# An attention and MLP block on one core: the last MLP block's results kept on chip, the rest of y fetched into the room of queries and keys, x and attention output loaded further ahead

## The chip, the cores and the metric

The kernel runs on one core of a Trainium2 chip. The core has TensorE (PE, matmuls, with its weight loads shown as PEld), VectorE (DVE), ScalarE (ACT), GpSimd (POOL) and SyncE (SP), which here only issues transfers; 16 DMA engines carry these between device memory and the on-chip memory (SBUF). Matmuls write accumulators (PSUM). The metric is the device time of one execution in microseconds; the median of several runs counts.

## What is computed

```python
B, S, D, H, W, F = 1, 2048, 640, 32, 256, 1536          # 20 columns per head

def attention(x, wqkv, wo):
    qkv = (x @ wqkv).reshape(B, S, 3, H, D // H).transpose(2, 0, 3, 1, 4)
    q, k, v = qkv[0], qkv[1], qkv[2]
    scores = jnp.einsum("bhqd,bhkd->bhqk", q, k) * (D // H) ** -0.5
    mask = (i - j >= 0) & (i - j < W)                    # sliding window, i query, j key
    p = softmax(jnp.where(mask, scores, -1e9))
    o = jnp.einsum("bhqk,bhkd->bhqd", p, v)
    return o.transpose(0, 2, 1, 3).reshape(B, S, D) @ wo

def mlp(x, w1, b1, w2, b2):
    r = relu(x @ w1 + b1)
    return (r * r) @ w2 + b2

xn = layernorm(x)
out = x + attention(xn, wqkv, wo) * silu(mlp(xn, w1, b1, w2, b2))
```

All is float32. Every product is made of three matmuls in a reduced format: each operand is split into a high part and a rest, and high x high, high x rest and rest x high are summed.

## The kernel before

Rows of x come in 16 tiles t of 128 and in four blocks b of four tiles. A first phase normalises x, turns it, keeps the turned blocks in device memory (xs) and makes V and the first queries and keys. The rest runs under a hand-written order: whatever Python emits first stands first on its engine, and each engine works through its own list in that order.

**The attention loop** (`for s in range(steps)`) runs over 16 pairs of heads p and 16 tiles q, with lags for the second pass over the scores and for the values. Pair p uses the buffers `qs[p % 2]` and `ks[p % 2]`, each 128 x 2048; pair 15, the last, uses `qs1` and `ks1`, so `qs0` and `ks0` lie unused from the end of pair 14 on. Exponents of scores lie in eight buffers `p32`. What a pair gives is stored to device memory as `o_d[g]`, one for each of four groups g of query tiles, and the sums that it must be divided by stand in it as additional rows.

**The filler** (`filler`) is a generator whose matmuls are put between those of the attention, up to a pace (`fill`). It makes the remaining queries and keys, and then the MLP in eight blocks n = (hf, b): for hf = 0 the first half of F over all blocks b, stored as `y_d[0]`; for hf = 1 the second half, to which the first is added (`yin`, loaded from `y_d[0]`), stored as `y_d[1]`. The second half goes over the blocks 2, 3, 0 and 1; the last block (n == last) holds the tiles 4 to 7. Its eight accumulations (four tiles tt, two halves nh of 320 columns) are evicted by DVE into `ysb` (`evac`). Ahead of each of them `late(j)` is called, which loads attention output of unit 0, and, where the attention loop is over (`state[2]` is then 10 ** 6), does more.

**The output stage** (`out_filler`) follows with eight units u of two tiles each (`tile_of`: 0 and 2, 1 and 3, 4 and 6, 5 and 7, and so on). Unit u belongs to group g = u // 2 and needs

- the attention output `ob` of its 256 query columns and the reciprocals of the sums (`sums`), issued by `load(u)`: four transfers of 160 KB and one of 128 KB. The reciprocals are made by `invert`: the rows of sums of a group are loaded as `rec`, DVE inverts them, and they are stored to `rec_d[g]`;
- `turn_out(u, 0)`, in which DVE multiplies `ob` by `sums` and ACT copies it into the high part of `oT`, and `turn_out(u, 1)`, in which DVE subtracts to get the rest, each in two pieces (columns of chunks 0 and 1, then 2 to 4);
- y of its two tiles, `yb`, one transfer of 640 KB issued at the end of `load(u)`, over which ACT then applies Silu;
- x of its tiles, `xres`, 320 KB each (`load_res`), one tile ahead of use.

For each tile and each half nh, 15 matmuls `wops` (L599) run into one of the three accumulators mm0 to mm2, DVE multiplies them by y into `res` (`evac`), POOL adds x, and SP stores `res`. The matmuls of the first tile of unit u are emitted after the turning out of unit u + 1 has begun, so on DVE the multiplication for unit u + 1 stands ahead of the evictions of unit u.

SP issues all transfers from one list. In the built program every transfer is bound to one of eight semaphores in turn, and waits for the transfer eight places ahead of it to land; besides it waits for its data and its buffer.

Of the kernel before, what the change touches and what calls it, by code (L numbers as in the profile page):

```python
# [15 lines left out]
P = 128  # L16
# [41 lines left out]
def attn_mlp_kernel(ctx: ExitStack, tc, x, wqkv, wo, w1, b1, w2, b2, out):  # L58
# [56 lines left out]
    qs = [at.tile([P, S], F32R, name="qs0")]  # L115
    ks = [at.tile([P, S], F32R, name="ks0")]
# [293 lines left out]
    qs.append(at1.tile([P, S], F32R, name="qs1"))  # L410
    ks.append(at1.tile([P, S], F32R, name="ks1"))
# [415 lines left out]
    def filler():  # L827
# [50 lines left out]
        def late(j):  # L878
            load(0)
            if state[2] < 10 ** 6:  # L880
                return
            invert()
            start_pieces()
            for f in release(1, True):
                f()
                held[0] -= 1
            if j >= 5:
                turn_out(0, 0)
            if j >= 6:
                turn_out(0, 1)  # L890
                load(1)

        for n, (hf, b) in enumerate(blocks):
# [54 lines left out]
            for tt in range(4):  # L948
# [4 lines left out]
                def start(nh, hf=hf, t=t, place=place, idx=4 * (n - NB) + tt, end=n == NB - 1 and tt == 3, n=n, tt=tt):  # L953
# [3 lines left out]
                    def evac():  # L957
                        vload[0] += 0.5
                        if not nh:
                            place[0] = wgt.tile([P, D], F32, tag="wgqh", name="ysb")  # L960
# [3 lines left out]
                        if nh:  # L964
                            post(y_d[hf][:, t, :], ysb)
# [20 lines left out]
                for nh in range(2):  # L986
                    yield from room()
                    if n == last:
                        late(2 * tt + nh)
# [24 lines left out]
    def invert():  # L1014
        for g in range(NB):
            if state[2] < stored(g) + 3:
                return
            rows = o_d[g].rearrange("p (h r) n -> (p h) r n", h=2)
            if g not in recs:
                recs[g] = at2.tile([P, P], F32, tag="rec", name="rec")  # L1020
                for par in range(2):
                    nc.sync.dma_start(recs[g][64 * par:64 * (par + 1)], rows[:, 32 * par + DH].rearrange("h (j n) -> h j n", n=P))
                return
            if recs[g] is not None and state[2] >= stored(g) + 5:
                nc.vector.reciprocal(recs[g], recs[g])
                nc.sync.dma_start(rec_d[g].rearrange("a h (j n) -> (a h j) n", n=P), recs[g])
                recs[g] = None

    def load(u):
        if u in ld or u >= 2 * NB or recs.get(u // 2, 0) is not None:  # L1030
            return
        if u % 2 == 0:
            obs[u // 2] = [bigp.tile([P, KC * BT], F32, tag="big", name=f"{w}_{u // 2}") for w in ("ob", "yb")]
        ob, yb = (t_[:, u % 2 * 2 * D:(u % 2 + 1) * 2 * D] for t_ in obs[u // 2])
        ob, yb = ob.rearrange("p (c n) -> p c n", c=KC), yb.rearrange("p (t d) -> p t d", t=2)
        sums = at2.tile([P, MT], F32, tag="sums", name="sums")
# [4 lines left out]
        t = tile_of(u, 0)  # L1041
        nc.sync.dma_start(yb, y_d[1][:, t:t + 3:2, :])
        ld[u] = (ob, yb, sums)

    obs, oT, turned_out = {}, {}, set()

    def turn_out(u, part):
# [3 lines left out]
        ob, _, sums = ld[u]  # L1051
# [7 lines left out]
        else:  # L1059
            for cs in cuts:  # L1060
                nc.vector.tensor_sub(oT[u][:, 1, cs], ob[:, cs], f32(oT[u][:, 0, cs]))

# [11 lines left out]
    def out_filler(wo_part):  # L1074
        xts = {}

        def load_res(t):
# [145 lines left out]
```

## Time and profile before

| | |
|---|---|
| median of 3 runs | 876.19 us (874.11 to 877.67) |
| the profiled execution | 874.52 us, its span 872.8 us, mean granted TensorE clock 0.994 |
| PE busy | 851.0 us (98%) |
| PEld busy | 795.2 us (91%) |
| DVE, ACT, POOL busy | 447.5, 422.7, 319.7 us |
| moved by DMA | 169.11 MB, mean 194 GB/s |

The span is the time from the first to the last instruction of the profiled execution; the rest of its time lies around it. A row of the timeline gives the start and the length of a run of equal instructions in us, the engine, the line of the source, the operation, what it writes and reads, shape and count, and in brackets how long the engine was idle ahead of it and what ended that. A row of the stretches gives busy time and count of instructions for PE, PEld, DVE, ACT and POOL, the granted clock, the share of the DMA engines and GB/s. SPq is SP's queue: its rows are issues, not transfers.

### The profile page before, as it was taken

The numbers are of one execution on the slowest core, as the hardware profiler recorded it, in microseconds if no ns is written. First come the engines' busy times: TensorE is split into PE (matmuls) and PEld (weight loads), VectorE is DVE, ScalarE is ACT, GpSimd is POOL, SyncE is SP. The second block draws the span as 40 slices with busy tenths as digits, with TensorE's granted clock in tenths as the row PEclk, the third lists the DMA queues.
The fourth block names the chain that finished last, engine by engine and source line by source line (L and its number), as shares of the span: only waits on it lengthen the run. The fifth ranks groups of instructions, "written<-read, shape, count | busy, mean of one in ns | idle before, by whom it ended". The sixth has DMA issues, their size and how long they took to land.

```text
span 872.8 us, 26498 instructions
## 1 busy us (share of the span) xinstructions
PE 851.0 (98%) x10640; PEld 795.2 (91%) x10640; DVE 447.5 (51%) x1348; ACT 422.7 (48%) x800; POOL 319.7 (37%) x652
## 2 busy tenths in 40 slices
PE   9999999999999999999999999999999999999787
PEld 8999999888888999999999989999999999889786
DVE  7652146656567555454454466454454454235443
ACT  5222114545557744745735756735736636622221
POOL 6010002333333543543634533634534534403232
PEclk9999999999999999999999999999999999999999
DMA  7997587778789373273475255474474452478995
GB/s 269 297 401 285 174 222 251 255 255 265 246 266 308 91 227 106 62 231 94 115 213 160 66 170 160 140 219 121 133 239 114 144 192 75 105 192 220 243 254 171
DMA packets 95394, 169.11 MB, mean 194 GB/s; under 512 B 10920, under 2 KB 43816, under 8 KB 94248
## 3 DMA queue, kind: packets, MB, share of 16 engines
q1 hardware_dynamic: 95272, 167.42, 63.5%
q8 instruction: 84, 1.38, 0.7%
q14 instruction: 38, 0.31, 0.1%
HBM read 94.97 MB, written 71.83 MB: 191 GB/s over the span
## 4 chain that ended last, share of the span: by engine, by line
PE 87%; DMA 7%; DVE 2%; issue 2%; ACT 1%; POOL 1%; SPq 0%; DVEq 0%; POOLq 0%
PE yps L468 20%; PE hps L468 20%; PE qkps L468 14%; PE ops L546 10%; PE vps L228 8%; PE stps L518 5%; PE sps L478 4%; PE qkps L205 3%; DMA xres<-in_A_x_dram 2%; DMA sums<-rec 2%; DMA out_dram<-res 1%; DMA yb<-y 1%; PE wops L599 1%; PE tps L172 1%; POOL res L1121 1%
## 5 line engine op out<-in xcount | busy, mean ns | idle before, releaser
L486 DVE CUSTOM_DVE_ANT_0 junk<-sps,mask 128x384 bf16<-128x384 f32 (+2 forms) x512 | 272.6, 532 | 249.2 <-PE hps L468 72.7
L524 ACT ACTIVATE p<-stps 128x768 f32<-128x768 f32 (+2 forms) x256 | 197.3, 771 | 261.4 <-PE stps L518 211.4
L468 PE MATMUL yps<-w,hh 64*128 64x320 f32 x1536 | 231.0, 311 | 3.6 <-DVE ysb L962 3.2
L525 POOL TENSOR_SCALAR_AFFINE_SELECT p<-p 128x256 f32<-128x256 f32 x256 | 105.6, 412 | 334.2 <-ACT p L524 325.6
L468 PE MATMUL hps<-xb,w 64*128 64x256 f32 x2520 | 220.8, 283 | 0.0
L468 PEld LDWEIGHTS hps<-xb,w 64*128 64x128 f32 x2520 | 209.0, 187 | 5.5 <-issue 5.4
L468 PEld LDWEIGHTS yps<-w,hh 64*128 64x128 f32 x1536 | 186.5, 186 | 8.2 <-DVE ysb L962 4.7
L468 PE MATMUL yps<-w,hl 64*128 64x320 f32 x768 | 178.3, 311 | 0.0
L478 PE MATMUL sps<-ks,qs 60*128 60x384 f32 (+2 forms) x512 | 142.6, 341 | 0.3
L518 PE MATMUL stps<-qs,ks 62*128 62x384 f32 (+2 forms) x512 | 135.6, 332 | 0.0
L468 PEld LDWEIGHTS yps<-w,hl 64*128 64x128 f32 x768 | 117.3, 186 | 2.4 <-issue 2.3
L468 PE MATMUL qkps<-xT,wgkh 64*128 64x512 f32 x320 | 100.5, 395 | 0.0
L468 PE MATMUL qkps<-xT,wgqh 64*128 64x512 f32 x320 | 98.9, 393 | 0.0
L546 PE MATMUL ops<-p,vp 128*21 128x128 f32 (+1 forms) x2112 | 92.8, 313 | 0.0
L527 POOL TENSOR_SCALAR_AFFINE_SELECT p<-p 128x256 f32<-128x256 f32 x224 | 91.4, 408 | 0.0
L478 PEld LDWEIGHTS sps<-ks,qs 60*128 60x128 f32 x512 | 87.8, 185 | 2.6 <-DVE mt L486 1.3
L518 PEld LDWEIGHTS stps<-qs,ks 62*128 62x128 f32 x512 | 88.7, 188 | 0.4
L546 PEld LDWEIGHTS ops<-p,vp 128*21 128x21 f32 x2112 | 65.2, 100 | 22.1 <-issue 9.0
L599 PE MATMUL wops<-wo,oT 128*128 128x320 f32 x384 | 65.0, 319 | 11.6 <-DVE res L1116 9.5
L599 PEld LDWEIGHTS wops<-wo,oT 128*128 128x128 f32 x384 | 59.8, 195 | 13.6 <-DVE res L1116 10.6
L228 PE MATMUL vps<-wv,xT 128*128 128x320 f32 x480 | 71.5, 308 | 0.0
L228 PEld LDWEIGHTS vps<-wv,xT 128*128 128x128 f32 x480 | 70.5, 188 | 0.1
(100 smaller groups left out, 1160.0 us busy)
## 6 DMA issues: line engine op xcount, KB each, us to landing
ks<-k_d SPq DMA_DIRECT2D x64, 240.0 KB
qs<-q_d SPq DMA_DIRECT2D x64, 240.0 KB
xb<-xs SPq DMA_DIRECT2D x60, 256.0 KB
xs<-xT SPq DMA_DIRECT2D x8, 1280.0 KB
y<-ysb SPq DMA_DIRECT2D x32, 320.0 KB
k_d<-shm SPq DMA_DIRECT2D x19, 512.0 KB
q_d<-shm SPq DMA_DIRECT2D x19, 512.0 KB
o<-osb SPq DMA_DIRECT2D x64, 128.0 KB
```

The lines of the kernel that those rows point to most:

```text
L172: nc.tensor.transpose(ps[:, t * P:(t + 1) * P], xns[t][:, c * P:(c + 1) * P], ident)
L205: nc.tensor.matmul(ps, wt[:, c, :], xT[part][b][:, c * BT + t0:c * BT + t0 + n], start=m == 1, stop=m == 3 * KC)
L228: nc.tensor.matmul(ps, xT[xp][b][:, c * BT + t * P: c * BT + (t + 1) * P], wv[wp][:, c, nh * HALF:(nh + 1) * HALF], start=first and m == 0 ...
L468: return nc.tensor.matmul(out, a[r], b_[r], skip_group_check=True, **kw)
L478: nc.tensor.matmul(ss[hh][:, :nk], qs[i][o, q * P:(q + 1) * P], ks[i][o, k0 * P:k0 * P + nk], start=True, stop=True)
L486: nc.vector.tensor_tensor_reduce(out=junk[:, :nk], in0=ss[hh][:, :nk], in1=mask[:, 3 * P - nk:], scale=1.0, scalar=-3.0e38, op0=ALU.add, o ...
L518: nc.tensor.matmul(tps[:, hh, :n], ks[i][o, kb * P:(kb + 1) * P], qs[i][o, kb * P:kb * P + n], start=True, stop=True)
L524: nc.scalar.activation(p32[:, :, :n], tps[:, :, :n], AF.Exp, scale=SCALE)
L525: nc.gpsimd.affine_select(p32[:, :, 0:P], p32[:, :, 0:P], pattern=[[0, 2], [1, P]], compare_op=ALU.is_ge, fill=0.0, base=0, channel_multip ...
L527: nc.gpsimd.affine_select(p32[:, :, 2 * P:], p32[:, :, 2 * P:], pattern=[[0, 2], [-1, P]], compare_op=ALU.is_gt, fill=0.0, base=0, channel ...
L546: nc.tensor.matmul(ot[r0:r0 + VW, c0:c0 + len(part), :], vps[p][:, kb // 4, kb % 4, hh, :], pt[:, hh, :].rearrange("p (t n) -> p t n", n=P ...
L599: nc.tensor.matmul(ps, a, b_, start=j == 0, stop=j == n - 1)
```

## The change

In the last MLP block `ysb` goes into a `p32` buffer and isn't stored: it stays on chip until the output stage uses it (`ybt[t]`). The other twelve tiles of y come by single loads of 320 KB into slices of `qs0`, `ks0`, `qs1` and `ks1` (`fetch_y`): six during the last steps of the attention loop into the room of pair 14, six into that of pair 15. `load(u)` no longer loads y, may be called for units up to u + 3, and takes every second `sums` from the buffers of `osb`. x gets six buffers, two `wgkh` and four of `p32`, and is loaded five tiles ahead. Silu is applied to one tile at a time, for unit u right after `turn_out(u, 1)`, for unit 0 at the start of the output stage. `late` counts its calls after the end of the loop itself.

```diff
-        def late(j):
+        def late():
             load(0)
             if state[2] < 10 ** 6:
                 return
-            invert()
+            j = lates[0]
+            lates[0] += 1
             start_pieces()
             for f in release(1, True):
                 f()
                 held[0] -= 1
+            invert(j)
+            for _ in range(2):
+                fetch_y()
+            if j >= 2:
+                load(1)
+            if j == 3 or j == 5:
+                load_res()
+            if j >= 4:
+                turn_out(0, 0)
             if j >= 5:
-                turn_out(0, 0)
-            if j >= 6:
                 turn_out(0, 1)
-                load(1)
...
-                            place[0] = wgt.tile([P, D], F32, tag="wgqh", name="ysb")
+                            place[0] = room_of("p32", "ysb") if n == last else wgt.tile([P, D], F32, tag="wgqh", name="ysb")
...
-                            post(y_d[hf][:, t, :], ysb)
+                            if n == last:
+                                ybt[t] = ysb
+                            else:
+                                post(y_d[hf][:, t, :], ysb)
...
-    def invert():
+    def invert(j=99):
         for g in range(NB):
-            if state[2] < stored(g) + 3:
+            over = state[2] >= 10 ** 6
+            if not over and state[2] < stored(g) + 3:
                 return
...
-                return
-            if recs[g] is not None and state[2] >= stored(g) + 5:
+            elif recs[g] is not None and (state[2] >= stored(g) + 5 if not over else j >= 2 + g % 2):
...
+    y_early = [((8 + j) % NT, w, i, j % 3) for j, (i, w) in enumerate([(i, w) for i in range(2) for w in "qk" for _ in range(3)])]
+    y_room = []
+
+    def fetch_y():
+        if y_early:
+            t, w, i, k = y_early.pop(0)
+            if not k:
+                y_room.append((at, at1)[i].tile([P, S], F32, tag=f"{w}s{i}", name=f"y{w}{i}"))
+            slot = y_room[-1][:, k * D:(k + 1) * D]
+            nc.sync.dma_start(slot, y_d[1][:, t, :])
+            ybt[t] = slot
+
+    in_order = [tile_of(u, t2) for u in range(2 * NB) for t2 in range(2)]
+    xts = {}
+
+    def load_res():
+        k = len(xts)
+        if k < NT:
+            t = in_order[k]
+            xts[t] = room_of("p32" if k % 3 else "wgkh", "xres")
+            nc.sync.dma_start(xts[t], x[t * P:(t + 1) * P, :])
...
-        sums = at2.tile([P, MT], F32, tag="sums", name="sums")
+        sums = at2.tile([P, 2, P], F32, tag="osb" if u % 2 else "sums", name="sums").rearrange("p a n -> p (a n)")
...
-        t = tile_of(u, 0)
-        nc.sync.dma_start(yb, y_d[1][:, t:t + 3:2, :])
...
+            if whole[0]:
+                silu(u)
+
+    def silu(u):
+        if u in shone:
+            return
+        shone.add(u)
+        for t2 in range(2):
+            yb = ybt[tile_of(u, t2)]
+            nc.scalar.activation(yb, yb, AF.Silu)
...
-        load_res(0)
+        while y_early:
+            fetch_y()
+        while len(xts) < 4:
+            load_res()
+        silu(0)
         for u in range(2 * NB):
...
-            load(u + 1)
             flush()
-            turn_out(u, 0)
-            turn_out(u, 1)
-            yb = ld[u][1]
-            nc.scalar.activation(yb, yb, AF.Silu)
+            if (u, 1) not in turned_out:
+                turn_out(u, 0)
+                turn_out(u, 1)
             for t2 in range(2):
                 t = tile_of(u, t2)
-                xt = xts.pop(t)
+                load_res()
...
-                    load(u + 1)
-                    load(u + 2)
+                    for v in range(u + 1, u + 4):
+                        load(v)
...
+            if s >= NP * NT - NT + LAG + 2 and len(ybt) < 6:
+                fetch_y()
```

The order of instructions shows where this puts things. SP's list from the last store of attention output on (o_88 and o_86 are o_d[3] and o_d[1], rec_1361 is rec_d[2], y_84 is y_d[1]), before:

```order
L564 DMA o_88<-osb 128x256
L564 DMA y_84<-ysb 128x640
L1079 DMA xres<-in_A_x_dram 128x640
L1039 DMA ob_14260<-o_85 32x5x256 x4
L1040 DMA sums<-rec_1359 128x1x256
L1042 DMA yb_14261<-y_84 128x2x640
L564 DMA y_84<-ysb 128x640
L1079 DMA xres<-in_A_x_dram 128x640
L1026 DMA rec_1361<-rec 128x128
L1022 DMA rec<-o_88 64x1x128 x2
L1039 DMA ob_14691<-o_86 32x5x256 x4
L1040 DMA sums<-rec_1360 128x1x256
```

and now:

```order
L564 DMA o_88<-osb 128x256
L1056 DMA yq_14647<-y_84 128x640 x3
L1056 DMA yk_14651<-y_84 128x640 x3
L1067 DMA xres<-in_A_x_dram 128x640 x5
L1038 DMA rec_1361<-rec 128x128
L1035 DMA rec<-o_88 64x1x128 x2
L1078 DMA ob_14268<-o_85 32x5x256 x4
L1079 DMA sums<-rec_1359 128x1x256
L1078 DMA ob_14702<-o_86 32x5x256 x4
L1079 DMA sums<-rec_1360 128x1x256
```

The loads of unit 1 (ob from o_85) stood ahead of the store of the third reciprocals (rec_1361) and stand behind it now, with six loads of y and five of x ahead of it.

ACT's list around its first copy for the output stage (oT_14653 and oT_14665 are unit 0's, oT_14662 and oT_14717 unit 1's), before:

```order
L551 ACTIVATE osb<-ops 128x256
L1058 ACTIVATE oT_14653<-ob_14260 128x512
L1058 ACTIVATE oT_14653<-ob_14260 128x768
L1093 ACT_TABLE_LOAD
L1093 ACTIVATE yb_14261<-yb_14261 128x1280
L1058 ACTIVATE oT_14662<-ob_14260 128x512
```

and now:

```order
L551 ACTIVATE osb<-ops 128x256
L1108 ACT_TABLE_LOAD
L1108 ACTIVATE yq_14647<-yq_14647 128x640
L1108 ACTIVATE yk_14651<-yk_14651 128x640
L1095 ACTIVATE oT_14665<-ob_14268 128x512
L1095 ACTIVATE oT_14665<-ob_14268 128x768
L1095 ACTIVATE oT_14717<-ob_14268 128x512
```

The table load and the Silu of tiles 0 and 2 stood behind unit 0's copies and stand ahead of them now; they read the late loads yq and yk.

DVE's list from unit 0's subtractions to unit 1's, now (before, unit 1's multiplication stood ahead of this reciprocal and the first eviction, and its subtractions right behind that eviction):

```order
L1098 TENSOR_TENSOR oT_14665<-ob_14268,oT_14665 128x512
L1098 TENSOR_TENSOR oT_14665<-ob_14268,oT_14665 128x768
L1037 RECIPROCAL rec<-rec 128x128
L1157 TENSOR_TENSOR res<-wops,yq_14647 128x320
L1094 TENSOR_TENSOR ob_14268<-ob_14268,sums 128x512
L1094 TENSOR_TENSOR ob_14268<-ob_14268,sums 128x768
L1037 RECIPROCAL rec<-rec 128x128
L1157 TENSOR_TENSOR res<-wops,yq_14647 128x320
L1157 TENSOR_TENSOR res<-wops,yk_14651 128x320 x2
L1098 TENSOR_TENSOR oT_14717<-ob_14268,oT_14717 128x512
L1098 TENSOR_TENSOR oT_14717<-ob_14268,oT_14717 128x768
```

Between unit 1's multiplication (ob by sums) and its subtractions there are now a reciprocal and three evictions of unit 0. TensorE's list has the same rows in the same order in both programs.

42 lines of the change are left out of this document (21 added, 21 removed).

## The prediction

> **What bounds the kernel now.** I read the page first, then the busy time by stretch, TensorE's timeline over the end of the run, and the rows of the engines that release it there.
>
> ```profile
> span 872.8 us, 26498 instructions
> PE   9999999999999999999999999999999999999787
> ```
>
> TensorE is full for 37 of 40 slices; only the last three have holes, and in them runs the output stage (wops, L599), the part that the change touches. So the stage from about 781 us on sets what can be won.
>
> ```profile
> 783.08 0.56 PE L599 MATMUL wops<-wo,oT 128*128 128x320 f32 x2 [1.84 <-ACT oT L1058]
> 787.45 1.92 PE L599 MATMUL wops<-wo,oT 128*128 128x320 f32 x12
> 794.04 1.92 PE L599 MATMUL wops<-wo,oT 128*128 128x320 f32 x12
> 811.66 2.02 PE L599 MATMUL wops<-wo,oT 128*128 128x320 f32 x12 [2.06 <-DVE res L1116]
> 823.73 2.60 PE L599 MATMUL wops<-wo,oT 128*128 128x320 f32 x12 [3.00 <-DVE res L1116]
> 829.78 1.92 PE L599 MATMUL wops<-wo,oT 128*128 128x320 f32 x12
> 866.00 1.92 PE L599 MATMUL wops<-wo,oT 128*128 128x320 f32 x12
> 868.05 0.31 PE L599 MATMUL wops<-wo4h,oT 128*128 128x320 f32 x1
> ```
>
> Each of the eight units u has four groups of 15 matmuls. From 787.45 to 794.04 three groups pass: **2.20 us a group**, 8.8 a unit. Unit 1 starts at 794.04 and the last group at 866.00. That is 27 groups, 59.4 us at full pace, in 71.96: **12.6 us are lost in units 1 to 7**. Part of it is a slow clock after the longest hole (823.73 to 829.78: 6.05 us for two groups instead of 4.4, so 1.65). Whatever ends TensorE's work at 868.36, the span ends 4.4 later (the last evictions and the last store).
>
> The rows name DVE's evictions (res), but these sit behind DVE's multiplication of the next unit's attention output by its sums, which waits for a transfer:
>
> ```profile
> 797.16 1.56 DVE L1057 TENSOR_TENSOR ob<-ob,sums 128x512 f32<-128x512 f32 x2 [2.42 <-DMA sums<-rec]
> 809.65 1.56 DVE L1057 TENSOR_TENSOR ob<-ob,sums 128x512 f32<-128x512 f32 x2 [6.11 <-DMA sums<-rec]
> 854.62 1.56 DVE L1057 TENSOR_TENSOR ob<-ob,sums 128x512 f32<-128x512 f32 x2 [5.78 <-DMA sums<-rec]
> ```
>
> ```profile
> 733.00:748.00 15.00, 15.00 (x246) 14.45 (x245) 5.09 (x18) 12.08 (x26) 9.19 (x17) 1.00 0.07 21
> 790.40:797.20 6.80, 6.80 (x48) 6.80 (x48) 2.40 (x6) 0.00 (x0) 2.61 (x3) 1.00 0.96 224
> 809.60:854.60 45.00, 37.48 (x240) 36.69 (x240) 18.89 (x32) 10.56 (x12) 13.80 (x16) 0.96 1.01 248
> ```
>
> The last two numbers are the share of the DMA engines and GB/s. From 809.6 to 854.6 four units pass, **11.25 us each**, with the transfers full (1.01) and TensorE busy for 37.5 of 45. So the transfers set the pace: a unit needs 8.8 us of matmuls and 11.25 us of transfers (2.75 MB: attention output 4 x 160 KB, sums 128, y 640, x 640, result 640).
>
> **What it removes.** Every unit loses its y load of 640 KB. What that is worth depends on the rate:
>
> ```profile
> DMA  0076899501007039969999999999999995220031
> GB/s 0 0 77 118 282 405 379 167 15 33 0 0 262 0 128 394 210 210 370 347 262 172 244 211 221 205 269 262 221 227 307 410 415 205 102 102 10 27 105 49
> ```
>
> These are half microseconds from 770 on. Loads and stores of 640 columns peak at about 400 (772.5, and again at 785.5), the stretches with attention output and sums lie at 172 to 270. At 400 the 0.655 MB are 1.64 us, so a unit falls to 11.25 - 1.64 = 9.6 us of transfers. Still above 8.8, but the change also pulls loads ahead: attention output and sums of units up to three ahead instead of two, x five tiles ahead. Counting transfers up to the last sums: before, they land at 854.6; minus seven y loads (11.5), minus two y stores of 320 KB (1.6; four go in all), plus six late y fetches (4.9), and by the order of SP's instructions two result stores that now come after them (-1.6) and one x load more ahead of them (0.8): about 845.6. By the terms below unit 6 starts on TensorE at 799.45 + 0.8 + 5 x 8.8 = 844.3, and its fourth group (the three accumulators mm0 to mm2 take the first three) needs the eviction that stands behind unit 7's multiplication (1.56): the sums may land as late as 844.3 + 6.6 - 1.6 = 849.3. So transfers stop setting the pace, by a margin of some 4 us, and the 12.6 us go. **Term 1: -12.6.**
>
> The six y tiles fetched in the attention loop move 1.97 MB between about 733 and 748, where the transfers stand at 0.07; the row above covers them. TensorE's order of instructions is the same, DVE's, ScalarE's and GpSimd's up to 781 too. If the cover fails, the row loads behind them (qs<-mrow) are late by one transfer, 0.8 us, and the exponent pass runs several steps behind the row loads, so I take zero; at worst +1.
>
> **What it adds: the start.** The new calls in late (fetch two y, load x, turn out unit 0 early) stand behind the test for the end of the main loop. In the order of instructions all six late y fetches and five x loads stand together ahead of unit 1's loads, and turn_out(0) still follows the last ysb on DVE: the block's eight groups are all started before the loop ends, so nothing of late's tail runs. And the Silu of unit 0 (tiles 0 and 2) now stands on ScalarE ahead of its copy of oT for unit 0, waiting for the third and fifth of those y.
>
> ```profile
> 775.19 0.33 SPq L564 DMA_DIRECT2D o<-osb  x1
> 776.51 0.33 SPq L564 DMA_DIRECT2D y<-ysb  x1
> 776.89 0.42 SPq L1079 DMA_DIRECT2D xres<-in_A_x_dram  x1
> 777.36 1.95 SPq L1039 DMA_DIRECT2D ob<-o  x4
> 779.35 0.56 SPq L1040 DMA_DIRECT2D sums<-rec  x1
> 788.10 0.32 SPq L1026 DMA_DIRECT2D rec<-rec  x1
> 788.47 1.17 SPq L1022 DMA_DIRECT2D rec<-o  x2
> 789.74 1.97 SPq L1039 DMA_DIRECT2D ob<-o  x4
> ```
>
> ```profile
> 782.39 0.63 ACT L1058 ACTIVATE oT<-ob 128x512 fp32r<-128x512 f32 x1 [7.23 <-DVE ob L1057]
> 784.14 0.96 DVE L1061 TENSOR_TENSOR oT<-ob,oT 128x768 fp32r<-128x768 f32 x1 [0.31 <-ACT oT L1058]
> 784.13 1.28 ACT L1093 ACT_TABLE_LOAD   x1
> 785.42 1.27 ACT L1093 ACTIVATE yb<-yb 128x1280 f32<-128x1280 f32 x1
> 787.13 0.94 DVE L1025 RECIPROCAL rec<-rec 128x128 f32<-128x128 f32 x1
> 792.16 0.83 DVE L1116 TENSOR_TENSOR res<-wops,yb 128x320 f32<-128x320 f32 x2
> ```
>
> The y fetches follow the store of 775.19, so bytes flow from about 776.4. Up to the fifth y it is 0.13 + 5 x 0.328 = 1.77 MB: 4.4 us at 400, a microsecond of ramp (the slices 77, 118, 282) and landing, so 782.4. The table load waits for none of them and runs while ScalarE is idle. A Silu over 640 columns is half of 1.27, 0.63, so the copy of oT starts at 783.05 instead of 782.39. **Term 2: +0.7**; 0 if y lands by 781.7, +4.6 at 172 GB/s (786.9).
>
> **What it moves: unit 1's loads.** Before, they are issued from 777.36, ahead of the store of the third reciprocals (788.10). Now they stand behind that store, which waits for the reciprocal on DVE, which waits for both subtractions of unit 0. The second subtraction ends at 785.5 (785.1 before; its copy starts 0.4 later), the reciprocal at 786.4, so that store goes out 1.7 us earlier than before. Behind it follow in both orders the loads of the fourth reciprocals and four loads of attention output, now unit 1's instead of unit 2's. Before, issue of these to the multiplication took 789.74 to 797.16, 7.4 us. So unit 1's multiplication starts at 788.05 + 7.4 = 795.45.
>
> Behind it on DVE stand the reciprocal (0.9), three evictions (1.25 from two in 0.83) and the two subtractions (0.6 and 0.95). Unit 1's first group can use its ninth matmul's operand 1.5 + 0.9 + 1.25 + 1.55 = 5.2 us after 795.45 and needs seven more matmuls (1.0), so it runs as if started at 795.45 + 6.2 - 2.2 = 799.45. Unit 0 ends at 794.04 + 0.7 = 794.74. **Term 3: +4.7**, a hole that the kernel before doesn't have. Its low end is 0 (loads that land by 790), its high end is the rivals' matter.
>
> A hole of 3.5 us without any matmul can bring the slow clock: after 3.00 us of idling it cost 1.65, after 2.06 nothing. **Term 4: +0.8**, between 0 and 1.65. For units 2 to 7 I leave **+0.5** (term 5; 0, or about 4 if the margin above is used up).
>
> Sum: -12.6 + 0.7 + 4.7 + 0.8 + 0.5 = **-5.9 us**. The profiled execution's span of 872.8 becomes 866.9. It took 874.52 in all, the median of the runs is 876.19; against the median I predict **870.3 us**.
>
> The Trainium skill (DMA: Bandwidth & Descriptors, Specifications) puts line rate at runs of 512 B and more, with a ceiling of 435 GB/s. Attention output moves in runs of 1 KB, and the slices above at 172 to 270 speak against it. By that page unit 1's 0.79 MB would be an estimated 1.8 us plus its fixed 2, so term 3 would shrink by about 2 and the result would be 868.
>
> **The rivals.** *The queue ahead of unit 1 drains slowly.* Eleven transfers and the store, 3.74 MB, stand ahead of its loads. At the 224 GB/s of the row of 790.40 they end at 793.1, not before the loads' issue; with 6.6 us from first bytes to the multiplication (7.4 less 0.8 from issue to bytes) it starts at 799.7, 4.2 later: -1.7, **874.5 us**. For it: the whole end of the run shows 224 to 248. Against: those are means with attention output in them; y and x run at 400.
>
> *The same on the other side.* If y and x go at 172, they end at 798.1 and unit 1 is multiplied at 804.7, 9.2 later: +3.3, **879.5 us**. It decides from where the queue drains below 203 GB/s (3.74 MB by 794.75). No y load in the row of slices is that slow by itself, but here eleven go in a row with no more than eight in flight.
>
> *Transfers never set the pace*: the share of 1.01 could be queues that wait, and the holes come from the order of issue. Then term 1 is nothing, and the new start and hole (+0.7 and +4.7) are all that stays: 881.6 us. By that page's rule it would be so, since 2.75 MB at 435 GB/s are an estimated 6.3 us, under 8.8. The rows speak against it: where sums were awaited, the slices were full.
>
> *It does all it says*: without the hole ahead of unit 1 it would be -12.6 + 0.7, some 864.3. The order of instructions rules it out but for a rest.
>
> **Chances.** The forecast 0.58, slow queue 0.24, slower still 0.10, no pace from transfers 0.03, the full gain 0.05. A measurement here tells 0.5% (4.4 us) from no change. The forecast gives up 0.04 to no change: faster 0.59, same 0.28, slower 0.13. The range goes from 867 (no slow clock, a shorter hole) to 878 (most of the slow queue); the forecast's own is 867.5 to 873.
>
> **What would show it.** Right: no y loads after the six at 776; the first wops near 783.7; a hole ahead of unit 1 that ends about 798 to 800 with DVE's multiplication behind sums; after it groups at 2.20 us without holes, and TensorE done near 862.5. Wrong: holes of 1 to 3 us before units 3 to 7 as before (term 1), the first wops after 785 (term 2), or unit 1's multiplication after 797 (term 3).

## The result and the profile after

The changed kernel takes **871.76 us** (median of 9 runs, 868.91 to 874.11), the kernel before 875.60 (9 runs, 873.15 to 878.05): a ratio of **0.9957, 95% interval 0.9937 to 0.9978**, some 3.8 us. The two profiled executions differ by 2.0 in their spans; that of the change lies 0.9 above its median, that of before 1.1 below. The forecast was 870.3 with a range from 867 to 878. The interval stays below 1, so a gain is there. By the prediction's own bound of 0.5% a gain of 0.43% still counts as no change, to which it gave 0.28 (faster 0.59); the interval reaches to both sides of that bound.

The page of the profile after: the span, and TensorE's busy time in 40 slices.

```profile
span 870.8 us, 26507 instructions
PE   9999999999999999999999999999999999997998
```

Of the three slices with holes, one thin slice and a dip at the end are left. TensorE's timeline, in the form used above (start, length, and in brackets what ended the idle time ahead):

```profile
785.34 3.76 PE L599 MATMUL wops<-wo,oT 128*128 128x320 f32 x12 [3.77 <-ACT oT L1095]
794.79 1.92 PE L599 MATMUL wops<-wo,oT 128*128 128x320 f32 x12
800.88 0.53 PE L599 MATMUL wops<-wo,oT 128*128 128x320 f32 x2 [3.73 <-DVE res L1157]
802.29 3.04 PE L599 MATMUL wops<-wo,oT 128*128 128x320 f32 x10 [0.88 <-DVE oT L1098]
805.92 2.99 PE L599 MATMUL wops<-wo,oT 128*128 128x320 f32 x12
809.19 1.92 PE L599 MATMUL wops<-wo,oT 128*128 128x320 f32 x12
864.19 1.92 PE L599 MATMUL wops<-wo,oT 128*128 128x320 f32 x12
```

And two stretches of it (the columns are PE, PEld, DVE, ACT, POOL, the granted clock, the share of the DMA engines and GB/s):

```profile
807.00:808.00 1.00, 1.00 (x5) 1.00 (x5) 1.00 (x2) 1.00 (x2) 1.00 (x1) 0.50 1.11 293
809.20:866.00 56.80, 56.80 (x390) 56.80 (x389) 34.02 (x47) 13.69 (x20) 25.98 (x25) 1.00 0.68 180
```

From 809.19 to 864.19 stand 25 groups in 55.0 us, 2.20 each: not one hole from the third group of unit 1 to the end, where the kernel before lost 12.6 us. What was paid for it stands ahead of 809.19: the first wops come at 785.34 (before: 783.08), and between the end of unit 0 near 797 and 809.19, 12.2 us pass for two groups that take 4.4 at full pace, the last of it at half the clock (0.50 in the row of 807). On DVE, ScalarE and SP's queue:

```profile
775.54 0.33 SPq L564 DMA_DIRECT2D o<-osb  x1
778.84 4.09 SPq L1067 DMA_DIRECT2D xres<-in_A_x_dram  x5
781.61 0.49 DVE L969 TENSOR_TENSOR ysb<-yps,yin 128x320 f32<-128x320 f32 x1 [2.09 <-PE yps L468]
784.03 0.74 ACT L1108 ACTIVATE yk<-yk 128x640 f32<-128x640 f32 x1 [2.40 <-DMA yk<-y]
784.67 1.35 ACT L1095 ACTIVATE oT<-ob 128x512 fp32r<-128x512 f32 x2
786.93 0.95 DVE L1037 RECIPROCAL rec<-rec 128x128 f32<-128x128 f32 x1
787.90 0.33 SPq L1038 DMA_DIRECT2D rec<-rec  x1
789.48 2.21 SPq L1078 DMA_DIRECT2D ob<-o  x4
797.97 1.56 DVE L1094 TENSOR_TENSOR ob<-ob,sums 128x512 f32<-128x512 f32 x2 [7.54 <-DMA ob<-o]
801.45 2.33 DVE L1098 TENSOR_TENSOR oT<-ob,oT 128x512 fp32r<-128x512 f32 x2
```

The chain is to be read downwards: ScalarE waits until 784.03 for the fifth late y and only then copies oT. The reciprocal follows the subtractions, its store goes out at 787.90, the loads of unit 1 go out behind it, and DVE multiplies at 797.97.

### The profile page after: what moved, and what is told of

Same layout as the page of the kernel before. It is cut to its first block, busy times and chain, and to the rows that moved or that the text cites. A ratio compares the mean times of both kernels' runs of the same rounds, so it can differ in the third digit from the quotient of the medians.

```text
span 870.8 us, 26507 instructions
## 1 busy us (share of the span) xinstructions
PE 852.4 (98%) x10640; PEld 796.1 (91%) x10640; DVE 456.1 (52%) x1348; ACT 423.1 (49%) x808; POOL 323.5 (37%) x652
## 4 chain that ended last, share of the span: by engine, by line
PE 93%; DMA 2%; DVE 2%; ACT 1%; issue 1%; SPq 1%; DVEq 0%
PE yps L468 20%; PE hps L468 20%; PE qkps L468 14%; PE ops L546 10%; PE vps L228 8%; PE wops L599 7%; PE stps L518 5%; PE sps L478 4%; PE qkps L205 3%; DMA ob<-o 1%; PE tps L172 1%; DMA yk<-y 1%; SPq L1078 0%; DVE junk L486 0%; DMA xt<-in_A_x_dram 0%
## 5 line engine op out<-in xcount | busy, mean ns | idle before, releaser
L527 POOL TENSOR_SCALAR_AFFINE_SELECT p<-p 128x256 f32<-128x256 f32 x224 | 91.5, 409 | 0.0
L599 PEld LDWEIGHTS wops<-wo,oT 128*128 128x128 f32 x384 | 62.1, 202 | 9.4 <-ACT oT L1095 8.0
```

The lines of the kernel that those rows point to most:

```text
L527: nc.gpsimd.affine_select(p32[:, :, 2 * P:], p32[:, :, 2 * P:], pattern=[[0, 2], [-1, P]], compare_op=ALU.is_gt, fill=0.0, base=0, channel ...
L599: nc.tensor.matmul(ps, a, b_, start=j == 0, stop=j == n - 1)
```

## The experiments

The last eviction ysb (L969) shown above ends the MLP. It comes between 779.96 and 783.68 in the builds, so the last column counts the span from its start; this is what the output stage alone takes. One profiled execution stands behind each of the last three columns. The kernels were timed in groups, each beside runs of the kernel before (medians 874.53 to 875.94).

| kernel | median us (runs) | ratio to before, 95% | span | last ysb | span from there |
|---|---|---|---|---|---|
| before | 875.60 (9) | | 872.8 | 781.27 | 91.5 |
| the change | 871.76 (9) | 0.9957 (0.9937 to 0.9978) | 870.8 | 781.61 | 89.2 |
| e1 | 869.28 (4) | 0.9945 (0.9924 to 0.9966) | 866.9 | 780.00 | 86.9 |
| e2 | 867.02 (4) | 0.9915 (0.9896 to 0.9934) | 865.3 | 780.65 | 84.7 |
| e3 | 863.79 (4) | 0.9882 (0.9860 to 0.9903) | 861.7 | 781.44 | 80.3 |
| e4 | 862.53 (4) | 0.9866 (0.9844 to 0.9889) | 859.7 | 780.44 | 79.3 |
| e5 | 875.70 (10) | 1.0005 (0.9989 to 1.0021) | 873.1 | 780.19 | 92.9 |
| e6 | 880.09 (7) | 1.0050 (1.0029 to 1.0072) | 878.4 | 782.35 | 96.1 |
| e7 | 863.35 (4) | 0.9871 (0.9842 to 0.9900) | 861.6 | 780.23 | 81.4 |
| e8 | 863.67 (4) | 0.9879 (0.9846 to 0.9913) | 861.6 | 780.54 | 81.1 |
| e9 | 863.53 (5) | 0.9876 (0.9855 to 0.9896) | 859.4 | 783.68 | 75.7 |
| e10 | 870.55 (4) | 0.9943 (0.9924 to 0.9963) | 870.4 | 781.76 | 88.6 |
| e11 | 872.74 (1) | one run | 871.0 | 782.46 | 88.5 |
| e12 | 859.81 (5) | **0.9810** (0.9790 to 0.9831) | 858.3 | 779.96 | 78.3 |

### e1, e2, e3: the start and the hole ahead of unit 1

e1 leaves the early Silu out (it then comes in turn_out), e2 puts unit 1's loads ahead of the late y, e3 does both.

```diff
     def out_filler(wo_part):
+        load(1)                     # e2 and e3
         while y_early:
             fetch_y()
         while len(xts) < 4:
             load_res()
-        silu(0)                     # e1 and e3
```

> Silu of unit 0 goes back behind its subtraction; all else is the changed kernel. Theory (the late start is ScalarE waiting for the fifth late y at 784.03, and unit 1's loads wait for the store of the third reciprocals, which DVE makes after unit 0's subtractions): the first wops of unit 0 comes 1.9 us earlier, near 783.4, the reciprocals and unit 1's multiplication move by the same 1.9, and the span falls by about 2 (870.8 to 869). Rival (unit 1 is held by what the DMA queues still have to drain, eleven y and x transfers, and not by the issue): unit 0 starts 1.9 earlier, but the multiplication of unit 1 stays at 798 within 0.5, the hole ahead of unit 1 grows by 1.9 and the span is the same within 0.5.

> The loads of unit 1 (four of attention output and the sums) are issued ahead of the six late y fetches; Silu of unit 0 stays ahead of the copy. Theory (7.8 us, the hole of some 5 and the slow clock around it, come from the place of unit 1's loads alone): the hole ahead of unit 1 vanishes, unit 1's multiplication stands near 790 instead of 798, and the late y and with it the first wops come about 3 us later (0.79 MB and 2.8 us of issue ahead of them): the span falls by some 4 to 5, to 866. Rival (the bytes in the queue are what holds unit 1, whatever their order): what unit 1 wins the start loses, and the span is the same within 1.

> Both edits: unit 1's loads ahead of the late y, and Silu of unit 0 behind its subtraction. Theory: the start is back near 783.4 (-1.9) and the hole ahead of unit 1 is gone (-7.8), so the span falls by 9 to 10, to about 861; the matmuls of the output stage then take 32 groups at 2.20 us with a slow clock of about 2 us in unit 0 alone. Rivals: if the order of issue doesn't matter and the bytes do, a hole of several us opens elsewhere in units 1 or 2 (y or x late) and the span stays above 866; if the two edits share one cause, the gain is that of the better one alone, 4 to 5.

The timeline of e1: the first wops, then the store, loads and multiplication of unit 1. Of e2: the first wops and unit 1's multiplication. Of e3: the first groups of the units 0 and 1.

```profile
781.81 0.55 PE L599 MATMUL wops<-wo,oT 128*128 128x320 f32 x2 [1.84 <-ACT oT L1095]
784.72 0.33 SPq L1038 DMA_DIRECT2D rec<-rec  x1
786.30 2.21 SPq L1078 DMA_DIRECT2D ob<-o  x4
794.78 1.56 DVE L1094 TENSOR_TENSOR ob<-ob,sums 128x512 f32<-128x512 f32 x2 [7.96 <-DMA ob<-o]
```

```profile
788.01 3.76 PE L599 MATMUL wops<-wo,oT 128*128 128x320 f32 x12 [7.40 <-ACT oT L1095]
789.60 1.55 DVE L1094 TENSOR_TENSOR ob<-ob,sums 128x512 f32<-128x512 f32 x2
```

```profile
783.25 3.84 PE L599 MATMUL wops<-wo,oT 128*128 128x320 f32 x12 [1.84 <-ACT oT L1095]
795.26 1.99 PE L599 MATMUL wops<-wo,oT 128*128 128x320 f32 x12
```

e1: counted from the last ysb, the multiplication moves from 16.4 to 14.8, and the output stage gains 2.3. Issue to multiplication takes 8.48 us in both (786.30 to 794.78, 789.48 to 797.97): unit 1 follows its store and isn't held by the queue's drain, so the rival falls. e2: the hole goes, the first wops come 3.6 later than in the change (7.36 behind the last ysb, against 3.73), and 4.5 us are won as forecast. e3 wins 8.9, just short of the 9 to 10 expected, and more than e1 and e2 together (6.8): with Silu behind the subtraction the later y no longer delay the start.

### e4, e5, e6: is it the bytes or the prefetch?

e4 keeps the y part alone; x and attention output are prefetched as in the kernel before, and the order is mended as in e3. e5 is e4, and e6 the change, with the 640 KB that y had taken put back for the units 1 to 7 as loads that nobody reads.

```diff
     def out_filler(wo_part):
-        while y_early:
-            fetch_y()
-        while len(xts) < 4:
-            load_res()
-        silu(0)
+        load_res()
...
+            load(u + 1)
+            while y_early:
+                fetch_y()
...
-                load_res()
...
+                    if nh == 0:
+                        load_res()
...
-                    for v in range(u + 1, u + 4):
-                        load(v)
+                    load(u + 1)
+                    load(u + 2)
```

```diff
     def load(u):
...
             obs[u // 2] = bigp.tile([P, KC * BT], F32, tag="big", name=f"ob_{u // 2}")
+            more[u // 2] = bigp.tile([P, KC * BT], F32, tag="big", name=f"more_{u // 2}")
...
+        t = tile_of(u, 0)
+        if u:
+            nc.sync.dma_start(more[u // 2][:, u % 2 * 2 * D:(u % 2 + 1) * 2 * D].rearrange("p (t d) -> p t d", t=2), y_d[0][:, t:t + 3:2, :])
```

> The y part of the change alone: the last MLP block's y stays on chip and the rest is fetched by single tiles, but x is loaded one tile ahead and attention output up to two units ahead, in the places of the kernel before, the six late y stand behind the loads of unit 1, and Silu of unit 0 behind its subtraction. Theory (what is won is the y loads taken out of a stage that transfers pace; further prefetch is worth nothing, and the start and the hole come from its order): start near 783.1 to 783.4, no hole ahead of unit 1, groups at 2.20 us after it: span 861 to 863. Rival (the holes of units 1 to 7 went because x and attention output come further ahead, not because there are fewer bytes): holes of 1 to 3 us ahead of units 3 to 7 as in the kernel before, span 868 to 872.

> e4 with the bytes put back: at the end of each of the loads of units 1 to 7, where the kernel before loads 640 KB of y, 640 KB of an older y are loaded into a buffer that nobody reads. Nothing waits for these loads but what stands behind them in the queues. Theory (transfers pace the output stage; the change wins by their bytes): units 2 to 7 lose their pace of 8.8 us again, DVE's multiplications wait for sums or attention output as in the kernel before, and the span goes from 859.7 to 870 to 876 (12.6 us of holes were lost to the same bytes before, and six late y, 4.9 us, come on top in the first units, less two y stores, 1.6). Rival (it was not the bytes, but that y no longer had to land before anything could be evicted): span 860 to 862.

> The changed kernel with the same dummy loads of 640 KB behind the sums of units 1 to 7. In the changed kernel the sums of unit 7 land near 842 and are needed by 852.9: 11 us of room, against 11.5 us of added transfers at the 400 GB/s of the slices. Theory (bytes pace the stage, and the prefetch gives room once): 0 to 3 us of holes, most of them in the last two units, span 871 to 874. Rival A (prefetch can't hide bytes at all): holes as in the kernel before, 10 us and more, span above 880. Rival B (bytes don't matter): span 870.8 within 0.5.

A stretch of e4 in the middle of the stage; then of e5 and of e6 the first and the last of the multiplications between which the transfers set the pace, and the stretch between them:

```profile
805.00:840.00 35.00, 35.00 (x238) 34.71 (x238) 21.47 (x32) 10.94 (x16) 15.23 (x16) 1.00 0.95 230
```

```profile
810.83 1.56 DVE L1098 TENSOR_TENSOR ob<-ob,sums 128x512 f32<-128x512 f32 x2 [5.84 <-DMA sums<-rec]
855.05 1.56 DVE L1098 TENSOR_TENSOR ob<-ob,sums 128x512 f32<-128x512 f32 x2 [5.92 <-DMA sums<-rec]
```

```profile
810.80:855.10 44.30, 38.18 (x242) 36.74 (x240) 19.54 (x33) 10.93 (x16) 13.71 (x16) 0.96 1.02 254
```

```profile
815.85 1.56 DVE L1098 TENSOR_TENSOR ob<-ob,sums 128x512 f32<-128x512 f32 x2 [2.87 <-DMA xres<-in_A_x_dram]
860.36 1.56 DVE L1098 TENSOR_TENSOR ob<-ob,sums 128x512 f32<-128x512 f32 x2 [5.73 <-DMA sums<-rec]
```

```profile
815.80:860.40 44.60, 39.64 (x262) 38.15 (x262) 21.47 (x33) 10.93 (x16) 15.23 (x16) 1.00 0.96 245
```

This settles the main question. e4 has no hole in that stretch (TensorE busy 35.00 of 35.00). Its output stage takes 79.3 where that of e3, with the mended order and the further prefetch, takes 80.3, so the further prefetch of x and attention output was worth nothing here. e5 differs from e4 by the added loads alone and is 13.6 us slower in the output stage (10 to 16 expected), back at the time of before. (Each added load is also one more transfer in a queue with eight in flight, and bytes and count were not varied apart; for the bytes speaks the engines' share of 1.02.) And e6 shows what prefetch can't do: from unit 3's multiplication on, four units take (860.36 - 815.85) / 4 = 11.1 us each, as in e5 (11.1) and before (11.25). The head start is used up by unit 3. It lost 6.9 us in the output stage, more than the 0 to 3 expected and less than rival A's 10. What was mis-sized there is the price of the added loads: they don't take 1.64 us each at 400 GB/s. With them a unit takes 11.1 us; without, the DMA engines carry one in 8.8 at a share of 0.95, so in an estimated 8.4. That makes **2.3 to 2.7 us** for the 0.655 MB, an estimate from e4, e5 and e6.

### e7, e8, e9, e12: towards a version without the holes

The tail of late would have turned unit 0 out ahead of the last evictions, but never runs. e7 does that in e4; e8 also fetches the tiles 0 to 3 early instead of 10 to 13; e9 also issues unit 1's loads right behind unit 0's, unit 2's earlier, and spreads the late y; e12 moves unit 1's loads to the last step of the attention loop.

```diff
+        if 0 in ld:                 # e7, e8, e9, e12
+            turn_out(0, 0)
+            turn_out(0, 1)
         drain(backlog)
...
-    y_early = [((8 + j) % NT, w, i, j % 3) for j, (i, w) in ...]
+    y_early = [(j if j < 4 else j + 4, w, i, j % 3) for j, (i, w) in ...]   # e8, e9, e12
...
             load(0)
+            if 0 in ld:             # e9 alone
+                load(1)
...
             load(u + 1)
-            while y_early:          # out in e9, e12 alone
-                fetch_y()
+            load(u + 2)             # e9, e12; fetch_y() follows each group
+            if u == 0:              # e7, e8, e9, e12
+                silu(0)
...
             invert()
+            if s == steps - 1:      # e12 alone
+                load(1)
```

> e4 with the turning out of unit 0 ahead of the last three evictions of the MLP block, which is what the new calls in late say and never do; Silu of unit 0 then stands at the start of the output stage. Theory (the 1.84 us without matmuls ahead of unit 0 are the turning out, and they bring the slow clock, 3.65 us for the first twelve matmuls instead of 1.92): the first wops follow the last yps without a gap, 1.84 + 1.73 = 3.6 us earlier; but the fifth late y lands as late as in e4, so the evictions of unit 0 wait for its Silu at 787.7 and 792.3 and a hole of 2 to 3.5 us opens within unit 0 or ahead of unit 1: net 0 to 1.5 won, span 858 to 860. Rival (the evictions are no limit): the whole 3.6, span 856.

> e7 with the early and late y changed: the six fetched in the attention loop are the tiles 0 to 3, 8 and 9, the late ones 10 to 15, so that units 0 and 1 wait for no late y. Theory: the whole 3.6 us of e7's start are won, no slow clock, groups at 2.20 from the first on; 32 groups are 70.4 us, and 4.4 follow: span 855 to 857. Rival (what e4 has as its first unit's slow clock is only the first use of new weights or operands, not the gap): the first twelve wops take 3.6 us here too, span 857 to 858.

> e8 with the order of transfers mended: attention output and sums of unit 1 are issued right behind those of unit 0, in the attention loop (sums of unit 1 from a buffer of sums, not of osb), those of unit 2 ahead of the store of the third reciprocals, and the late y one by one behind the groups of units 0 to 2. Theory (what e7 and e8 lost was DVE's multiplication for unit 1, which waits for sums until 786.2 and holds back the evictions of unit 0): the start without a gap as in e8, no hole of 1 us or more behind it, groups at 2.20 us: 32 groups are 70.4 us and 4.4 follow, a span of 855 to 857 and a ratio to the kernel before of 0.980 to 0.983. Rival (transfers of 160 KB that go earlier delay those of wo and of the reciprocals, and a hole opens ahead of unit 2 instead): span 859 to 862, as e4.

> e9 with unit 1's loads in another place: not behind those of unit 0 near 756.5, but at the last step of the attention loop, near 771, behind the last transfers of wo. Theory (e9 lost at the end of the MLP block what it won behind it: the wo transfers stood behind unit 1's loads, ScalarE's copy of wo waited for them until 767.4, and the last ysb came at 783.68 instead of 780.5): the last ysb is back near 780.5, the output stage keeps e9's pace without holes, and 75.7 us after the last ysb give a span of 856 to 857, a ratio of 0.980 to 0.983. Rival (the place of the last ysb moves by itself by a microsecond or two between builds, or unit 1's loads now delay the last store of o): last ysb at 782 or later, span 858 or more.

e8, TensorE and unit 1's multiplication:

```profile
781.18 1.99 PE L599 MATMUL wops<-wo,oT 128*128 128x320 f32 x12 [0.68 <-DVE ysb L969]
786.20 1.56 DVE L1097 TENSOR_TENSOR ob<-ob,sums 128x512 f32<-128x512 f32 x2 [5.17 <-DMA sums<-rec]
789.02 2.04 PE L599 MATMUL wops<-wo,oT 128*128 128x320 f32 x12 [1.01 <-DVE res L1162]
793.88 3.44 PE L599 MATMUL wops<-wo,oT 128*128 128x320 f32 x12 [2.37 <-DVE res L1162]
```

Both e7 and e8 missed what was expected of them: the start came without the gap of 1.84, but both are 2 us slower than e4 in the output stage. The wait that ends last has moved: DVE's multiplication for unit 1 waits for its sums until 786.20 (e7: 785.87), and the evictions of unit 0 stand behind it.

e9, ScalarE's wait for wo, the last ysb, and the first and last group:

```profile
767.38 0.74 ACT L773 ACTIVATE wo<-raw 128x640 fp32r<-128x640 f32 x1 [3.24 <-DMA raw<-in_A_wo_dram]
783.68 0.49 DVE L971 TENSOR_TENSOR ysb<-yps,yin 128x320 f32<-128x320 f32 x1 [2.09 <-PE yps L468]
784.32 1.99 PE L599 MATMUL wops<-wo,oT 128*128 128x320 f32 x12 [0.68 <-DVE ysb L971]
852.80 1.92 PE L599 MATMUL wops<-wo,oT 128*128 128x320 f32 x12
```

Its output stage has the pace that was aimed at: 31 groups from 784.32 to 852.80, 2.21 each. But the last ysb came 3.1 later than in e8. The loads that were put earlier delayed those of wo, as the rival had it, though the delay shows at another place than it named. That is not all of it: from 759.5 to 765 the clock was granted at 0.69 in e9 and at 1.00 in e8, which the section on the forecast finds to cost 1.5 us. From the start of the matmuls near 759 to the last ysb e9 takes 24.3 us, e8 20.9; so some 1.9 are left for wo. The profiled run is the fastest of five (861.16), so the median says more.

e12, the first group, and the one wait left, on both engines:

```profile
780.60 3.28 PE L599 MATMUL wops<-wo,oT 128*128 128x320 f32 x12 [0.68 <-DVE ysb L969]
813.96 1.56 DVE L1097 TENSOR_TENSOR ob<-ob,sums 128x512 f32<-128x512 f32 x2 [4.66 <-DMA sums<-rec]
815.98 2.02 PE L599 MATMUL wops<-wo,oT 128*128 128x320 f32 x12 [0.61 <-DVE res L1162]
```

The last ysb is back at 779.96, with no wait for wo and the clock at 1.00 from 759.5 to 765. The span is 858.3 instead of 856 to 857, for a slow first group and 1.2 us of holes at 816 and 818.6. The ratio of 0.981 is within what was expected, and e12 is the fastest kernel here, an estimated 1.5% under the change (0.9810 / 0.9957, two ratios of different groups).

### e10 and e11: the slow clock, and GpSimd beside DVE

e10 fills the hole ahead of unit 1 with 22 matmuls whose result nobody reads. e11 leaves out GpSimd's additions of x, so its output lacks x in all but the last tile.

```diff
+                    if u == 1 and not t2 and not nh:
+                        wm = pair_tile()
+                        for _ in range(22):
+                            nc.tensor.matmul(wm[:, 0, :HALF], wo_part(1, 0)[:, :P], wo_part(0, 0)[:, :HALF], start=True, stop=True)
                     ps = mm_bank([P, HALF], "wops")
```

```diff
-                        nc.gpsimd.tensor_add(res[:, sl], res[:, sl], xt[:, sl])
```

> The changed kernel with 22 matmuls of 128x320 whose result nobody reads, on TensorE between the last matmul of unit 0 and the first of unit 1 (some 3.2 us at 0.147, less than the 3.73 that it idles there). Theory (the hole costs twice: once as idling, once as the slow clock behind it; unit 1's second group ends 2.8 us later than the operands and full pace allow): the first matmuls of unit 1 start at the same time, but run at 0.147 instead of 0.27 us, and the span falls by 2 to 3. Rival (the slow first groups of unit 1 wait for their operands, which DVE makes in 2.33 us instead of 1.55): the span is the same within 0.5.

> The changed kernel without GpSimd's additions of x (the output lacks x in all but the last tile). Theory (DVE's 512 and 768 columns take 2.23 us where GpSimd adds at the same time, and 1.56 where it doesn't): the multiplications and subtractions of all units take 1.55 to 1.56 (1.70 for subtractions behind a copy), and the span moves by less than 1, since DVE has room in units 2 to 7; ahead of unit 1 it may win 0.5. Rival (DVE is slow because of ScalarE or of the DMAs' writes): they stay at 2.2.

e10 on TensorE, with the stretch in which the clock falls:

```profile
796.79 3.39 PE L1149 MATMUL stps<-wo,wo 128*128 128x320 f32 x22
802.30 1.15 PE L599 MATMUL wops<-wo,oT 128*128 128x320 f32 x6 [0.89 <-DVE oT L1098]
803.85 1.25 PE L599 MATMUL wops<-wo,oT 128*128 128x320 f32 x4 [0.40 <-DVE oT L1098]
805.70 2.74 PE L599 MATMUL wops<-wo,oT 128*128 128x320 f32 x12
```

```profile
804.00:805.00 1.00, 1.00 (x5) 1.00 (x6) 1.00 (x2) 0.00 (x0) 0.52 (x1) 0.55 0.89 208
```

A miss for the theory: 0.6 us are won in the output stage instead of 2 to 3. The clock stayed at full until 804, but six fast matmuls only reach the wait for the second subtraction (0.40) sooner. Then the clock fell to half all the same and slowed the second group. So the operands set the first group's pace, as the rival had it, and the slow clock the second's. What the hole would cost at full clock throughout was not reached.

e11, the subtractions and the multiplication that took 2.33 and 2.22 in the change:

```profile
802.19 1.55 DVE L1098 TENSOR_TENSOR oT<-ob,oT 128x512 fp32r<-128x512 f32 x2
803.66 1.55 DVE L1094 TENSOR_TENSOR ob<-ob,sums 128x512 f32<-128x512 f32 x2
```

As expected, the pairs are back at 1.55, and the span is the same (871.0; a single run).

## Why the forecast came near, and where its steps were off

The forecast was a gain of 5.9 us; 3.8 were measured between the medians, and 2.0 between the two profiled executions that the working is about. That it lies within 1.5 of the median is in part luck: on the trace the same sum misses by 4.

**Term 1 (-12.6) was right, and is shown.** The holes that the kernel before had in the units 1 to 7 are gone, and e4 against e5 gives the cause, the loads of y. Two steps on the way to it were off, in opposite directions: the y load was priced at 1.64 us from the peak slices and is worth an estimated 2.3 to 2.7, and the prefetch was counted as a help, which e4 shows isn't needed. The margin of "some 4 us" was larger than forecast: the sums of unit 7 are issued at 837.39, and DVE's multiplication at 849.54 waits for no transfer. Term 5 (+0.5) was 0. The rival by which transfers never set the pace is refuted by e5: at a share of 1.02 the stage moves 254 GB/s. The Trainium skill (DMA: Bandwidth & Descriptors, Specifications) puts line rate at runs of 512 B and more, with a ceiling of 435 GB/s; the measurement stands against it for this mix.

**Term 2 was mis-sized: +0.7 forecast, +1.9 measured** (last ysb to first wops, 3.73 against 1.81). The mechanism is right; in e1, without the early Silu, the first wops come 1.81 behind the last ysb, as before. The step that failed is the landing of the fifth y at 782.4, counted as if all bytes up to it came first; ScalarE waits for it until 784.03. The half-microsecond slices from 770 on:

```profile
GB/s 0 0 0 143 230 299 104 10 0 33 0 0 72 191 143 230 323 343 384 405 307 307 328 353 389 328 374 405 405 399 415 410 410 343 133 56 20 124 7 62
```

The sixteen slices from 776 to 784 sum to 2.44 MB, and the store and five y are 1.77. The other 0.67 MB went to what stands behind: here transfers in flight shared the rate. A fixed time from the last byte to the landing would not do: in order, the store and three y (1.11 MB) would be through near 780.2 by these slices, and ScalarE has the third y at 780.89; the 1.77 MB would be through near 782.2, and it has the fifth at 784.03. The lag grows from 0.7 to 1.8. (No run varied the number in flight, so the sharing is argued from the slices.) Unit 0 was slowed more than before by the clock, which was not in the sum: another 0.7 (785.34 to 797.0 is 11.65, before 10.96).

**Terms 3 and 4 were mis-sized: +5.5 together, +7.8 measured** (12.2 for two groups that need 4.4). The hole, its place and its cause are right: e2 removes it by the place of the loads alone. The multiplication came at 797.97 instead of 795.45: 1.4 from the later reciprocal (786.93 against 785.5) and 1.1 because issue to multiplication took 8.5, not the 7.4 of before. Behind it DVE's subtractions took 2.33 instead of 1.55, and the clock stood at half for most of two groups. By the prediction's own marks (first wops after 785, multiplication after 797) terms 2 and 3 are wrong. The misses add up: 1.2 of term 2, 0.7 of unit 0's clock, 2.3 of terms 3 and 4 and 0.3 of a later last ysb, less the 0.5 of term 5, are the 4 us by which the forecast for TensorE's end (862.5) missed the measured 866.5. Against the median the miss is 1.5, since the runs gained more than the two profiled executions.

**The free parts show no cost.** The last ysb comes between 780.00 and 782.35 in e1 to e6, which all have the six early fetches, at 781.61 in the change and at 781.27 before. Most of this scatter is the clock. Every profiled execution has a gap of 1.73 to 1.75 us on TensorE that ends between 758.85 and 760.55. Behind it the clock from 759.5 to 765 is granted at 0.69 before, in the change, e6, e9, e10 and e11, and at 1.00 in the others. From the end of the gap to the last ysb it takes 22.42 to 22.44 us in the first lot (e9, which also waits for wo, 24.32) and 20.88 or 20.89 in the second: 1.5 us for the clock, which the columns counted from the last ysb leave out. Before and the change fall in the same lot with the same 22.42, so what is left for the early fetches in this pair is at most the 0.3 by which the gap ends later. Late's tail is absent, and e7, e8, e9 and e12 show what turning out unit 0 early is worth, with and without the transfers in a fitting order.

**The rivals.** The slow queue (874.5) didn't come. By the slices above 3.73 MB have passed between 776 and 788, the store and all eleven loads, and the rate is down to 20 GB/s before unit 1's loads are issued at 789.48; and e1 shows unit 1 following its store. So the slower one (879.5) didn't come either.

## What to carry to other kernels

Where a stage is paced by transfers, bytes taken out count, at the rate of that stage's own mix and not at the peak; prefetch only gives a head start, which e6 used up in three units. Fetches that are needed late, put ahead of loads that are needed next, can cost most of the gain: here 8.9 us of the output stage, against the 12.6 of holes removed, were a matter of two lines of order. And after a wait is removed, look at what else stands in the same in-order list: e7 and e8 removed a gap of 1.84 and met the next wait 5 us later.

## What the runs showed of the hardware

**DVE beside GpSimd.** In the change DVE's pair of 512 and 768 columns takes 1.56 us alone and 2.22 to 2.33 while GpSimd adds. GpSimd's addition is stretched as well, here first beside such a pair and then alone:

```profile
806.81 1.25 POOL L1162 TENSOR_TENSOR res<-res,xres 128x320 f32<-128x320 f32 x1 [2.31 <-DVE res L1157]
809.96 0.89 POOL L1162 TENSOR_TENSOR res<-res,xres 128x320 f32<-128x320 f32 x1 [1.90 <-DVE res L1157]
```

The Trainium skill (SBUF — State Buffer, SBUF: two separate sides) says that a DVE instruction with two operands from SBUF and a GpSimd instruction that reads SBUF take turns for a shared pair of ports, one blocking the other. e11 agrees that it is GpSimd that slows DVE. In the kernel before the two seldom met: two of its sixteen pairs took over 2.2.

**The slow clock comes after short gaps too.** The first twelve matmuls of e8 and e12 (1.99 and 3.28 us) stand behind the same gap of 0.68. The rows of 781 to 784, e8 first, then e12:

```profile
781.00:784.00 3.00, 2.82 (x19) 2.85 (x20) 0.03 (x1) 0.00 (x0) 0.00 (x0) 1.00 1.08 222
```

```profile
781.00:784.00 3.00, 3.00 (x13) 3.00 (x13) 1.78 (x3) 2.68 (x4) 0.00 (x0) 0.50 1.05 177
```

The granted clock is 1.00 in one and 0.50 in the other, and e12 ran 13 matmuls where e8 ran 19. e7 was slow like e12 (3.20), e9 fast like e8 (1.99). Near 759, behind a gap of 1.73 to 1.75 us in all fourteen executions, six were slow. By rows of one microsecond the spell lasts some 3.4 us, near 759 in the kernel before as at 781 in e7 and e12. The Trainium skill (TensorE: Matmul & The Clock Gate, What's actually happening) has the clock set by windows of 3.4 us that run on freely. The length of these slow spells fits that, but by its rule a window must pass idle, and here a slow spell followed a gap of 0.67 or 0.68 us in two of four kernels. What decides between them stays open; it moves these kernels by 1.5 us.
